# A SwiGLU feed-forward kernel: row blocks of 384, 384, 384, 384 and 512 in place of four of 512

## The chip, the cores and the metric

One core of a Trainium2 chip. The time is device microseconds of one execution. The span of a profile runs from the first to the last instruction of one profiled execution; the time is a little longer. Kernels are compared only within the same rounds.

## The reference

```
x: (1, 2048, 640)   w_gate, w_up: (640, 1536)   w_down: (1536, 640)   all bf16
return (silu(x @ w_gate) * (x @ w_up)) @ w_down
```

## The kernel before

The work is done in row blocks. For each block, twelve steps (`fc`) of gate and up projections (five matmuls each, contraction 640 = 5 x 128) fill `aT`; ScalarE takes the silu of the gate, VectorE multiplies. Then one group `po_t` gives 128 of the 640 output columns in transposed form, and one group `po_a` per 128 rows the other 512.

```
S_BLK = 512; NSB = 4; SUB = 4
W_CHUNKS = [(0, 1), (1, 3), (3, 6), (6, 9), (9, 12)]      # slices in which w_gate and w_up are loaded
# SyncE queue: x chunks, weight slices, w_down, then
turn_x(1)                       # x of block 1, transposed by the DMA
x_row <- last four rows of x, broadcast
turn_w(wgT, wgt_v)              # w_gate transposed, three slices of four fc
```

The last four rows are not in the matmuls. They are computed by VectorE as 96 row dots of `wgT` and `wuT` with `x_row`, handed out between the other work by `do_dots(n)`. In the traces here VectorE, ScalarE, TensorE and the SyncE queue take their work one after the other in the order of the program (ScalarE, for example, casts the first `po_a` at 37.41 us, behind the four stores that it began to issue at 35.38). The loop, shortened:

```
for sb in range(NSB):
    for fc in range(KF):
        proj(pg, ...); proj(pu, ...)                       # PSUM tag "gu", 4 buffers
        silu on ScalarE, product on VectorE
        if sb > 0 and fc < KF - 2: do_dots(2)
    po_t = psum.tile(..., tag="po_b")                      # 2 buffers
    ... 12 matmuls ...
    nc.scalar.copy(ot_t, po_t)
    do_dots(3)
    nc.vector.transpose(out=ot_q, in_=ot_t)
    for q in range(4): nc.scalar.dma_start(out=out2[...], in_=ot_q[...])
    for j in range(SUB):
        po_a = psum.tile([P, DA], f32, tag="po_a")         # 2 buffers
        ... 12 matmuls ...
        nc.scalar.copy(ot, po_a)
        if 0 < j: do_dots(3)
        nc.sync.dma_start(out=out2[...], in_=ot)
    if sb == 0: turn_x(2); turn_w(wuT, wut_v); turn_x(3)
```

Of the kernel before, what the change touches and what calls it, by code (L numbers as in the profile page):

```python
# [10 lines left out]
def _body(  # L11
# [8 lines left out]
    nc = tc.nc  # L20
    P = nc.NUM_PARTITIONS
    f32 = mybir.dt.float32
    bf16 = mybir.dt.bfloat16
# [9 lines left out]
    KD = D // P  # L33
    KF = F // P
    S_BLK = 512
    NSB = S // S_BLK
    SUB = S_BLK // P
    DA = 512
    Q = 32
    N_WARM, N_GAP = 18, 2  # L40
    T = 4
    WT_STEP = 4
    ROW_J = 0
    W_CHUNKS = [(0, 1), (1, 3), (3, 6), (6, 9), (9, 12)]
    assert D % P == 0 and F % P == 0 and S % S_BLK == 0 and D > DA and SUB == 4

    consts = ctx.enter_context(tc.tile_pool(name="consts", bufs=1))
    work = ctx.enter_context(tc.tile_pool(name="work", bufs=3))
# [3 lines left out]
    )  # L52

    ident = consts.tile([P, P], bf16)
    x_sb = consts.tile([P, SUB, D], bf16)
    xT = consts.tile([P, KD, S], bf16)
    wg_sb = consts.tile([P, KD, F], bf16)
    wu_sb = consts.tile([P, KD, F], bf16)
# [24 lines left out]
    def load_x(eng, c0, c1):  # L83
        eng.dma_start(out=x_sb[:, c0:c1, :], in_=x_v[:, c0:c1, :])  # L84

    def issue_order(a, b):
        tc.add_manual_dep(
            b,
            a.name,
            mybir.DependencyInfo(  # L90
                mybir.DependencyClass.NoSync, mybir.DependencyReason.DATA
            ),
            reason="issue_order",
        )
# [8 lines left out]
    silu_first = consts.tile([P, 1], f32)  # L103
    nc.vector.memset(ones[:], 1.0)  # L104

    queues = (nc.sync, nc.scalar)
    halves = ((0, KD // 2 + 1), (KD // 2 + 1, KD))
    load_x(nc.sync, 0, 1)
    first = nc.cur_bb.bb.instructions[-1]
    load_x(nc.scalar, 2, 3)  # L110


    issue_order(first, nc.cur_bb.bb.instructions[-1])
    load_x(nc.sync, 1, 2)
    load_x(nc.scalar, 3, 4)
    for dst, src in ((wg_sb, wg_v), (wu_sb, wu_v)):
        for eng, (k0, k1) in zip(queues, halves):
            eng.dma_start(out=dst[:, k0:k1, wslice(0, 1)], in_=src[:, k0:k1, wslice(0, 1)])
    load_w(nc.sync, wg_sb, wg_v, *W_CHUNKS[1])
    nc.scalar.activation(silu_first[:], ones[:, 0:1], ACT.Silu)  # L120
# [6 lines left out]
    wut_v = w_up.rearrange("d (kf p) -> d kf p", p=P)  # L127

    def turn_x(sb):
        s_sl = slice(sb * S_BLK, (sb + 1) * S_BLK)  # L130
        nc.sync.dma_start_transpose(out=xT[:, :, s_sl], in_=xt_v[s_sl])

    def turn_w(dst, src):
        for a in range(0, KF, WT_STEP):
            nc.sync.dma_start_transpose(
                out=dst[:, a : a + WT_STEP, :], in_=src[:, a : a + WT_STEP, :]
            )
# [3 lines left out]
        out=x_row[:],  # L141
        in_=x2[S - T : S, :].rearrange("t d -> (t d)").partition_broadcast(P),
    )
    turn_w(wgT, wgt_v)

    def row_dots():

# [24 lines left out]
    def do_dots(n):  # L172
        for _ in range(n):
            next(dots, None)
# [3 lines left out]
    def warm(n):  # L178
        for _ in range(n):
            nc.tensor.matmul(  # L180
                pw[:, 0:P], lhsT=ones[:], rhs=ones[:], start=True, stop=True
            )

    def transpose_chunk(c, parts):
        c_sl = slice(c * P, (c + 1) * P)
        for copy, tag, k0, k1 in parts:
            pt = psum.tile([P, k1 - k0, P], bf16, tag=tag, name="pt")
            for kd in range(k0, k1):
                nc.tensor.transpose(  # L189
                    out=pt[:, kd - k0, :],  # L190
                    in_=x_sb[:, c, kd * P : (kd + 1) * P],
                    identity=ident[:],
                )
            copy(out=xT[:, k0:k1, c_sl], in_=pt[:])  # L194

    def proj(ps, w_sb, fc, sb, c0, c1):
        for kd in range(KD):
            nc.tensor.matmul(  # L198
                ps[:, c0:c1],
                lhsT=w_sb[:, kd, fc * P : (fc + 1) * P],  # L200
                rhs=xT[:, kd, sb * S_BLK + c0 : sb * S_BLK + c1],
                start=(kd == 0),
                stop=(kd == KD - 1),
            )

    def proj_pair(ps, w_sb, fc, sb, b):


        def pair(ap):
            return ap.rearrange("p (a b c) -> p b a c", b=2, c=P)[:, b]  # L210

        for kd in range(KD):
            nc.tensor.matmul(  # L213
                pair(ps[:]),
                lhsT=w_sb[:, kd, fc * P : (fc + 1) * P],
                rhs=pair(xT[:, kd, sb * S_BLK : (sb + 1) * S_BLK]),
                start=(kd == 0),
                stop=(kd == KD - 1),
            )

    for sb in range(NSB):
        n_s = S_BLK if sb < NSB - 1 else S_BLK - T
        s_sl = slice(sb * S_BLK, sb * S_BLK + n_s)
        for fc in range(KF):
            pg = psum.tile([P, S_BLK], f32, tag="gu", name="pg", bufs=4)
            pu = psum.tile([P, S_BLK], f32, tag="gu", name="pu", bufs=4)
            if sb == 0 and fc == 0:
                dve, act = nc.vector.tensor_copy, nc.scalar.copy
                warm(N_WARM)
                transpose_chunk(0, [(dve, "po_a", 0, KD)])  # L230
                transpose_chunk(2, [(dve, "po_b", 0, KD)])
                warm(N_GAP)
                for c in (1, 3):
                    transpose_chunk(c, [(act, "po_a", 0, 2), (dve, "po_b", 2, KD)])
                warm(2)
                proj_pair(pg, wg_sb, fc, sb, 0)
                proj_pair(pg, wg_sb, fc, sb, 1)
                proj(pu, wu_sb, fc, sb, 0, S_BLK)
                keep_order(mybir.EngineType.PE)
                keep_order(mybir.EngineType.Activation)  # L240
            else:
                proj(pg, wg_sb, fc, sb, 0, n_s)
                proj(pu, wu_sb, fc, sb, 0, n_s)
            sg = work.tile([P, S_BLK], f32)
            nc.scalar.activation(sg[:, 0:n_s], pg[:, 0:n_s], ACT.Silu)  # L245
            nc.vector.tensor_tensor(  # L246
                out=aT[:, fc, s_sl], in0=sg[:, 0:n_s], in1=pu[:, 0:n_s], op=ALU.mult
            )
            if sb > 0 and fc < KF - 2:
                do_dots(2)  # L250


        n_t = (SUB if sb < NSB - 1 else SUB - 1) * P
        po_t = psum.tile([P, n_t], f32, tag="po_b", name="po_t")
        for kf in range(KF):
            nc.tensor.matmul(  # L256
                po_t[:],
                lhsT=wd_sb[:, kf, DA:D],
                rhs=aT[:, kf, sb * S_BLK : sb * S_BLK + n_t],
                start=(kf == 0),  # L260
                stop=(kf == KF - 1),
            )
        ot_t = outp.tile([P, n_t], bf16, name="ot_t")
        ot_q = outp.tile([P, n_t], bf16, name="ot_q")
        nc.scalar.copy(ot_t[:], po_t[:])  # L265
        do_dots(3)
        nc.vector.transpose(out=ot_q[:], in_=ot_t[:])  # L267
        for q in range(P // Q):
            nc.scalar.dma_start(
                out=out2[  # L270
                    sb * S_BLK : sb * S_BLK + n_t, DA + q * Q : DA + (q + 1) * Q
                ].rearrange("(i r) c -> r i c", r=Q),
                in_=ot_q[q * Q : (q + 1) * Q, :].rearrange("r (i c) -> r i c", c=Q),
            )

        for j in range(SUB):
            s0 = sb * S_BLK + j * P
            last = sb == NSB - 1 and j == SUB - 1
            po_a = psum.tile([P, DA], f32, tag="po_a", name="po_a")
            for kf in range(KF):  # L280
                nc.tensor.matmul(  # L281
                    po_a[:],
                    lhsT=aT[:, kf, s0 : s0 + P],
                    rhs=wd_sb[:, kf, 0:DA],
                    start=(kf == 0),
                    stop=(kf == KF - 1),
                )
            ot = outp.tile([P, DA], bf16, name="ot")
            nc.scalar.copy(ot[:], po_a[:])  # L289
            if 0 < j:  # L290
                do_dots(3)
            if sb == NSB - 1 and j == ROW_J:
                row_tail()
            nc.sync.dma_start(out=out2[s0 : s0 + P, 0:DA], in_=ot[:])
            if last:
                po_b = psum.tile([P, D - DA], f32, tag="po_b", name="po_b")
                for kf in range(KF):
                    nc.tensor.matmul(  # L298
                        po_b[:],
                        lhsT=aT[:, kf, s0 : s0 + P],  # L300
                        rhs=wd_sb[:, kf, DA:D],
                        start=(kf == 0),
                        stop=(kf == KF - 1),
                    )
                ot_b = outp.tile([P, D - DA], bf16, name="ot_b")
                nc.vector.tensor_copy(out=ot_b[:], in_=po_b[:])  # L306
                nc.scalar.dma_start(out=out2[s0 : s0 + P, DA:D], in_=ot_b[:])
        if sb == 0:
            turn_x(2)
            turn_w(wuT, wut_v)  # L310
            turn_x(3)
    keep_order(mybir.EngineType.DVE)
    keep_order(mybir.EngineType.SP)

# [104 lines left out]
```

## Time and profile before

| | before |
|---|---|
| time, median of the first 3 runs | 163.87 us |
| span of the profile | 162.8 us |
| TensorE busy | 159.7 us (98%) |
| VectorE busy | 111.8 us (69%) |
| first gate matmul | 5.30 us |
| first slice of `wgT` lands / first dot | 31.0 / 32.1 us |

TensorE is busy from 5.3 us to 160.7, two microseconds before the end. In a timeline, the bracket at the end of a line gives the idle time of the engine ahead of it and what ended that.

### The profile page before, as it was taken

The numbers are of one execution on the slowest core, as the hardware profiler recorded it, in microseconds if no ns is written. First come the engines' busy times: TensorE is split into PE (matmuls) and PEld (weight loads), VectorE is DVE, ScalarE is ACT, GpSimd is POOL, SyncE is SP. The second block draws the span as 40 slices with busy tenths as digits, with TensorE's granted clock in tenths as the row PEclk, the third lists the DMA queues.
The fourth block names the chain that finished last, engine by engine and source line by source line (L and its number), as shares of the span: only waits on it lengthen the run. The fifth ranks groups of instructions, "written<-read, shape, count | busy, mean of one in ns | idle before, by whom it ended". The sixth has DMA issues, their size and how long they took to land.

```text
span 162.8 us, 2081 instructions
## 1 busy us (share of the span) xinstructions
PE 159.7 (98%) x779; PEld 75.4 (46%) x779; DVE 111.8 (69%) x251; ACT 42.6 (26%) x73; POOL 0.6 (0%) x6
## 2 busy tenths in 40 slices
PE   8999999999999999999999999999999999999994
PEld 7644444444444444444444444444444444445442
DVE  2223333499559999979919999979964999993000
ACT  3322222212232222221222322221214222222121
POOL 1000000000000000000000000000000000000000
DMA  7999999993269993003110000000420000000312
GB/s 212 295 327 330 364 216 253 245 185 60 66 152 180 220 220 68 4 0 34 64 64 0 0 4 2 0 0 0 64 68 32 0 0 0 0 0 4 53 35 73
DMA packets 42585, 15.86 MB, mean 97 GB/s; under 512 B 33232, under 2 KB 42448, under 8 KB 42576
## 3 DMA queue, kind: packets, MB, share of 16 engines
q1 hardware_dynamic: 33664, 14.75, 37.2%
q10 hardware_dynamic: 8912, 0.98, 4.0%
q8 instruction: 6, 0.10, 0.3%
q14 instruction: 3, 0.02, 0.1%
HBM read 7.21 MB, written 2.62 MB: 60 GB/s over the span
## 4 chain that ended last, share of the span: by engine, by line
PE 95%; DMA 3%; SPq 0%; DVE 0%; issue 0%
PE pu L198 32%; PE pg L198 31%; PE po_a L281 25%; PE po_t L256 6%; DMA wg_sb<-in_w_gate_dram 3%; PE pg L213 1%; SPq L84 0%; PE po_b L298 0%; DVE ot_b L306 0%
## 5 line engine op out<-in xcount | busy, mean ns | idle before, releaser
L198 PE MATMUL pu<-xT,wu_sb 128*128 128x512 bf16 (+1 forms) x240 | 59.5, 379 | 0.0
L198 PE MATMUL pg<-xT,wg_sb 128*128 128x512 bf16 (+1 forms) x235 | 58.3, 379 | 0.0
L246 DVE TENSOR_TENSOR aT<-sg,pu 128x512 bf16<-128x512 f32 (+1 forms) x48 | 32.8, 683 | 32.0 <-PE pu L198 32.0
L245 ACT ACTIVATE sg<-pg 128x512 f32<-128x512 f32 (+1 forms) x48 | 28.6, 596 | 70.2 <-PE pg L198 65.7
L281 PE MATMUL po_a<-wd_sb,aT 128*128 128x512 bf16 x192 | 42.1, 379 | 0.0
L151 DVE SCALAR_TENSOR_TENSOR prod<-wgT,x_row 128x640 f32<-128x640 bf16 x48 | 39.4, 821 | 1.1
L151 DVE SCALAR_TENSOR_TENSOR prod<-wuT,x_row 128x640 f32<-128x640 bf16 x48 | 39.4, 821 | 1.0
L198 PEld LDWEIGHTS <-wu_sb 128*128 128x128 bf16 x240 | 23.5, 98 | 28.0
L198 PEld LDWEIGHTS <-wg_sb 128*128 128x128 bf16 x235 | 23.0, 98 | 27.6
L281 PEld LDWEIGHTS <-aT 128*128 128x128 bf16 x192 | 18.8, 98 | 22.5
L289 ACT CAST ot<-po_a 128x512 bf16<-128x512 f32 x16 | 9.4, 586 | 32.3 <-PE po_a L281 21.3
L256 PE MATMUL po_t<-aT,wd_sb 128*128 128x512 bf16 (+1 forms) x48 | 10.4, 366 | 0.0
L256 PEld LDWEIGHTS <-wd_sb 128*128 128x128 bf16 x48 | 4.7, 98 | 5.1
L306 DVE CAST ot_b<-po_b 128x128 bf16<-128x128 f32 x1 | 0.3, 291 | 9.9 <-PE po_b L298 9.9
L265 ACT CAST ot_t<-po_t 128x512 bf16<-128x512 f32 (+1 forms) x4 | 2.2, 560 | 11.6 <-PE po_t L256 11.6
L194 DVE COPY xT<-pt 128x640 bf16<-128x640 bf16 (+1 forms) x4 | 1.6, 425 | 3.4 <-PE pt L189 3.4
L151 DVE DVE_READ_ACCUMULATOR prod<-wuT,x_row 128x1 f32 x48 | 3.9, 82 | 0.0
L151 DVE DVE_READ_ACCUMULATOR prod<-wgT,x_row 128x1 f32 x48 | 3.9, 82 | 0.0
L267 DVE STREAM_TRANSPOSE ot_q<-ot_t 128x512 bf16<-128x512 bf16 (+1 forms) x4 | 2.7, 678 | 1.7 <-ACT ot_t L265 1.7
L180 PE MATMUL pw<-ones 128*128 128x128 bf16 x22 | 2.8, 304 | 0.4 <-DVE ones L104 0.4
L189 PE MATMUL pt<-ident,x_sb 128*128 128x128 bf16 x20 | 2.0, 268 | 0.5 <-DMA x_sb<-in_x_dram 0.5
L180 PEld LDWEIGHTS <-ones 128*128 128x128 bf16 x22 | 2.2, 143 | 0.4 <-DVE ones L104 0.4
(17 smaller groups left out, 9.0 us busy)
## 6 DMA issues: line engine op xcount, KB each, us to landing
out_dram<-ot SPq DMA_DIRECT2D x16, 128.0 KB, 1.7
wd_sb<-in_w_down_dram SPq DMA_DIRECT2D x1, 1920.0 KB, 12.6
wg_sb<-in_w_gate_dram SPq DMA_DIRECT2D x3, 480.0 KB, 7.1
wu_sb<-in_w_up_dram SPq DMA_DIRECT2D x3, 480.0 KB, 7.6
x_row<-in_x_dram SPq DMA_DIRECT2D x1, 640.0 KB, 4.8
out_dram<-ot_q ACTq DMA_DIRECT2D x12, 32.0 KB, 1.9
x_sb<-in_x_dram SPq DMA_DIRECT2D x2, 160.0 KB, 3.0
x_sb<-in_x_dram ACTq DMA_DIRECT2D x2, 160.0 KB, 3.2
```

Source lines behind the costliest of these rows:

```text
L151: nc.vector.scalar_tensor_tensor(out=prod[:], in0=wT[:, fc, :], scalar=1.0, in1=x_row[:, t, :], op0=ALU.mult, op1=ALU.mult, accum_out=acc[ ...
L180: nc.tensor.matmul(pw[:, 0:P], lhsT=ones[:], rhs=ones[:], start=True, stop=True)
L189: nc.tensor.transpose(out=pt[:, kd - k0, :], in_=x_sb[:, c, kd * P : (kd + 1) * P], identity=ident[:],)
L198: nc.tensor.matmul(ps[:, c0:c1], lhsT=w_sb[:, kd, fc * P : (fc + 1) * P], rhs=xT[:, kd, sb * S_BLK + c0 : sb * S_BLK + c1], start=(kd == 0 ...
L213: nc.tensor.matmul(pair(ps[:]), lhsT=w_sb[:, kd, fc * P : (fc + 1) * P], rhs=pair(xT[:, kd, sb * S_BLK : (sb + 1) * S_BLK]), start=(kd == ...
L245: nc.scalar.activation(sg[:, 0:n_s], pg[:, 0:n_s], ACT.Silu)
L246: nc.vector.tensor_tensor(out=aT[:, fc, s_sl], in0=sg[:, 0:n_s], in1=pu[:, 0:n_s], op=ALU.mult)
L256: nc.tensor.matmul(po_t[:], lhsT=wd_sb[:, kf, DA:D], rhs=aT[:, kf, sb * S_BLK : sb * S_BLK + n_t], start=(kf == 0), stop=(kf == KF - 1),)
L265: nc.scalar.copy(ot_t[:], po_t[:])
L267: nc.vector.transpose(out=ot_q[:], in_=ot_t[:])
L281: nc.tensor.matmul(po_a[:], lhsT=aT[:, kf, s0 : s0 + P], rhs=wd_sb[:, kf, 0:DA], start=(kf == 0), stop=(kf == KF - 1),)
L289: nc.scalar.copy(ot[:], po_a[:])
```

## The change

The intent is a shorter head: a first block of three chunks needs one x load and five transposes less before its first matmul. The first weight slices are cut finer, since a smaller block wants them faster, and the last two `wgT` slices move behind the first block.

```diff
-    S_BLK = 512
+    SUBS = [3, 3, 3, 3, 4]                  # chunks of 128 rows
-    W_CHUNKS = [(0, 1), (1, 3), (3, 6), (6, 9), (9, 12)]
+    W_CHUNKS = [(0, 1), (1, 2), (2, 4), (4, 6), (6, 9), (9, 12)]
 ...
-    load_x(nc.scalar, 3, 4)                 # the fourth x chunk of the first block
 ...
-    turn_w(wgT, wgt_v)
+    turn_w(wgT, wgt_v, 0, WT_STEP)          # the first slice only
 ...
-            if sb > 0 and fc < KF - 2:
-                do_dots(2)
+            if sb > 0 and (SUBS[sb] == 3 or fc < KF - 2):
+                do_dots(SUBS[sb] - 2)
 ...
         if sb == 0:
+            turn_w(wgT, wgt_v, WT_STEP, KF)
             turn_x(2)
-            turn_w(wuT, wut_v)
+            turn_w(wuT, wut_v, 0, KF)
             turn_x(3)
+            turn_x(4)
```

Cut: the same index changes wherever a block is addressed; the first gate group, now chunks 0 and 2 and then chunk 1; which of the two queues loads which part of the very first weight slices; and a fixed issue order of the first two x loads, which is dropped.

More of the change, by code (lines that the diff above doesn't have):

```diff
@@ L35, in _body @@
     S_BLK = 512
-    NSB = S // S_BLK
-    SUB = S_BLK // P
+    SUBS = [3, 3, 3, 3, 4]
+    NSB = len(SUBS)
+    ROW0 = [sum(SUBS[:n]) * P for n in range(NSB)]
     DA = 512
@@ L43, in _body @@
     ROW_J = 0
-    W_CHUNKS = [(0, 1), (1, 3), (3, 6), (6, 9), (9, 12)]
-    assert D % P == 0 and F % P == 0 and S % S_BLK == 0 and D > DA and SUB == 4
+    W_CHUNKS = [(0, 1), (1, 2), (2, 4), (4, 6), (6, 9), (9, 12)]
+    assert D % P == 0 and F % P == 0 and S == sum(SUBS) * P and D > DA and max(SUBS) * P <= S_BLK
     consts = ctx.enter_context(tc.tile_pool(name="consts", bufs=1))
@@ L54, in _body @@
     ident = consts.tile([P, P], bf16)
-    x_sb = consts.tile([P, SUB, D], bf16)
+    x_sb = consts.tile([P, SUBS[0], D], bf16)
     xT = consts.tile([P, KD, S], bf16)
@@ L104, in _body @@
     nc.vector.memset(ones[:], 1.0)
-    queues = (nc.sync, nc.scalar)
-    halves = ((0, KD // 2 + 1), (KD // 2 + 1, KD))
     load_x(nc.sync, 0, 1)
-    first = nc.cur_bb.bb.instructions[-1]
     load_x(nc.scalar, 2, 3)
-    issue_order(first, nc.cur_bb.bb.instructions[-1])
     load_x(nc.sync, 1, 2)
-    load_x(nc.scalar, 3, 4)
-    for dst, src in ((wg_sb, wg_v), (wu_sb, wu_v)):
-        for eng, (k0, k1) in zip(queues, halves):
+    for dst, src, k in ((wg_sb, wg_v, 3), (wu_sb, wu_v, 2)):
+        for eng, k0, k1 in ((nc.scalar, 0, k), (nc.sync, k, KD)):
             eng.dma_start(out=dst[:, k0:k1, wslice(0, 1)], in_=src[:, k0:k1, wslice(0, 1)])
@@ L129, in turn_x, with turn_w @@
     def turn_x(sb):
-        s_sl = slice(sb * S_BLK, (sb + 1) * S_BLK)
+        s_sl = slice(ROW0[sb], ROW0[sb] + SUBS[sb] * P)
         nc.sync.dma_start_transpose(out=xT[:, :, s_sl], in_=xt_v[s_sl])
-    def turn_w(dst, src):
-        for a in range(0, KF, WT_STEP):
+    def turn_w(dst, src, lo, hi):
+        for a in range(lo, hi, WT_STEP):
             nc.sync.dma_start_transpose(
@@ L194, in transpose_chunk, with proj @@
             copy(out=xT[:, k0:k1, c_sl], in_=pt[:])
-    def proj(ps, w_sb, fc, sb, c0, c1):
+    def proj(ps, w_sb, fc, sb, n, cols=lambda ap: ap):
         for kd in range(KD):
             nc.tensor.matmul(
-                ps[:, c0:c1],
+                cols(ps[:, 0:n]),
                 lhsT=w_sb[:, kd, fc * P : (fc + 1) * P],
-                rhs=xT[:, kd, sb * S_BLK + c0 : sb * S_BLK + c1],
+                rhs=cols(xT[:, kd, ROW0[sb] : ROW0[sb] + n]),
                 start=(kd == 0),
@@ L204, in proj, with outer_chunks, mid_chunk @@
             )
-    def proj_pair(ps, w_sb, fc, sb, b):
-        def pair(ap):
-            return ap.rearrange("p (a b c) -> p b a c", b=2, c=P)[:, b]
-        for kd in range(KD):
-            nc.tensor.matmul(
-                pair(ps[:]),
-                lhsT=w_sb[:, kd, fc * P : (fc + 1) * P],
-                rhs=pair(xT[:, kd, sb * S_BLK : (sb + 1) * S_BLK]),
-                start=(kd == 0),
-                stop=(kd == KD - 1),
-            )
+    def outer_chunks(ap):
+        return ap.rearrange("p (c r) -> p c r", r=P)[:, 0:3:2]
+    def mid_chunk(ap):
+        return ap[:, P : 2 * P]
     for sb in range(NSB):
-        n_s = S_BLK if sb < NSB - 1 else S_BLK - T
-        s_sl = slice(sb * S_BLK, sb * S_BLK + n_s)
+        n_s = SUBS[sb] * P - (T if sb == NSB - 1 else 0)
+        s_sl = slice(ROW0[sb], ROW0[sb] + n_s)
         for fc in range(KF):
@@ L232, in _body @@
                 warm(N_GAP)
-                for c in (1, 3):
-                    transpose_chunk(c, [(act, "po_a", 0, 2), (dve, "po_b", 2, KD)])
-                warm(2)
-                proj_pair(pg, wg_sb, fc, sb, 0)
-                proj_pair(pg, wg_sb, fc, sb, 1)
-                proj(pu, wu_sb, fc, sb, 0, S_BLK)
+                transpose_chunk(1, [(act, "po_a", 0, 2), (dve, "po_b", 2, KD)])
+                warm(N_GAP)
+                proj(pg, wg_sb, fc, sb, n_s, outer_chunks)
+                proj(pg, wg_sb, fc, sb, n_s, mid_chunk)
+                proj(pu, wu_sb, fc, sb, n_s)
                 keep_order(mybir.EngineType.PE)
@@ L241, in _body @@
             else:
-                proj(pg, wg_sb, fc, sb, 0, n_s)
-                proj(pu, wu_sb, fc, sb, 0, n_s)
+                proj(pg, wg_sb, fc, sb, n_s)
+                proj(pu, wu_sb, fc, sb, n_s)
             sg = work.tile([P, S_BLK], f32)
@@ L248, in _body @@
             )
-            if sb > 0 and fc < KF - 2:
-                do_dots(2)
-        n_t = (SUB if sb < NSB - 1 else SUB - 1) * P
+            if sb > 0 and (SUBS[sb] == 3 or fc < KF - 2):
+                do_dots(SUBS[sb] - 2)
+        n_t = (SUBS[sb] if sb < NSB - 1 else SUBS[sb] - 1) * P
         po_t = psum.tile([P, n_t], f32, tag="po_b", name="po_t")
@@ L258, in _body @@
                 lhsT=wd_sb[:, kf, DA:D],
-                rhs=aT[:, kf, sb * S_BLK : sb * S_BLK + n_t],
+                rhs=aT[:, kf, ROW0[sb] : ROW0[sb] + n_t],
                 start=(kf == 0),
@@ L270, in _body @@
                 out=out2[
-                    sb * S_BLK : sb * S_BLK + n_t, DA + q * Q : DA + (q + 1) * Q
+                    ROW0[sb] : ROW0[sb] + n_t, DA + q * Q : DA + (q + 1) * Q
                 ].rearrange("(i r) c -> r i c", r=Q),
@@ L274, in _body @@
             )
-        for j in range(SUB):
-            s0 = sb * S_BLK + j * P
-            last = sb == NSB - 1 and j == SUB - 1
+        for j in range(SUBS[sb]):
+            s0 = ROW0[sb] + j * P
+            last = sb == NSB - 1 and j == SUBS[sb] - 1
             po_a = psum.tile([P, DA], f32, tag="po_a", name="po_a")
```

## The prediction

> **What bounds the kernel now.** I read the chain of work that ended last first, since it says which engine sets the end and where the end is not that engine.
>
> ```profile
> PE 95%; DMA 3%; SPq 0%; DVE 0%; issue 0%
> 0.91 4.35 DMA wg_sb<-in_w_gate_dram
> 5.30 1.27 PE pg L213 x10
> 31.39 2.59 PE po_t L256 x12
> 33.98 10.36 PE po_a L281 x48
> 147.74 1.95 PE po_t L256 x12
> 149.69 10.36 PE po_a L281 x48
> ```
>
> The kernel is a TensorE stream. It starts at 5.30 us, when the first gate weights have landed, and then runs without a hole until 160.7; the rest is the last copy and store. So there are two ways to move the time: start the stream earlier, or open a hole in it. The second matters as much as the first, so I next read what works beside TensorE at the end of the first row block, in the timeline:
>
> ```profile
> 31.50 0.69 DVE L246 TENSOR_TENSOR aT<-sg,pu 128x512 bf16<-128x512 f32 x1 [1.47 <-PE pu L198]
> 32.10 0.82 DVE L151 SCALAR_TENSOR_TENSOR prod<-wgT,x_row 128x640 f32<-128x640 bf16 x1
> 34.63 0.71 DVE L267 STREAM_TRANSPOSE ot_q<-ot_t 128x512 bf16<-128x512 bf16 x1
> 35.38 1.99 ACTq L269 DMA_DIRECT2D out_dram<-ot_q  x4
> 37.41 0.59 ACT L289 CAST ot<-po_a 128x512 bf16<-128x512 f32 x1 [2.81 <-DMA out_dram<-ot_q]
> ```
>
> This is a chain of its own. VectorE does three row dots (32.10 to 34.63), then its transpose; ScalarE issues the stores of the transposed tile only after that (35.38), and only then casts the first `po_a` (37.41). `po_a` has two buffers, so the third group of `po_a` matmuls waits for that cast. Before, the cast ends at 38.00 and the third group is due at 33.98 + 2 x 2.59 = 39.16: a slack of 1.2 us that the chain of waits never shows. Last I read when the dots' inputs arrive, from the SyncE timeline and the list of DMA issues:
>
> ```profile
> 10.66 1.43 SPq L125 DMA_DIRECT2D wd_sb<-in_w_down_dram  x1
> 12.13 11.32 SPq L131 DMA_TRANSPOSE xT<-in_x_dram  x1
> 23.50 0.57 SPq L140 DMA_DIRECT2D x_row<-in_x_dram  x1
> 24.12 4.39 SPq L135 DMA_TRANSPOSE wgT<-in_w_gate_dram  x1
> wgT<-in_w_gate_dram SPq DMA_TRANSPOSE x1, 6.9
> ```
>
> The first slice of `wgT` lands at 24.12 + 6.9 = 31.0 us. VectorE wants it at 32.10. So the dots do not wait today, by 1.1 us. The table by windows shows why it cannot come much sooner: the DMA engines are at a busy share of about 1.0 to 1.2 from 2 us to 20 us, at 255 to 364 GB/s, and the SyncE queue sends everything in order: x, weights, `wd`, transposed x, `x_row`, `wgT`.
>
> **What the Trainium skill says.** "TensorE: Matmul & The Clock Gate", section "Wait — 56ns, not 53.3ns?", gives N / 2.4 GHz + 2.5 ns from matmul to matmul: 216 ns at 512 columns, 162.5 at 384. The trace agrees: 2.59 us / 12 = 216 ns, and the last block's `po_t` of 384 columns 1.95 / 12 = 162.5 ns. "PSUM — Partial Sum Buffer", section "Engine vs sequencer instructions", says that ScalarE and VectorE queues are strict FIFO and that matmuls start in program order. The trace agrees: ScalarE stood 2.81 us behind its store with a finished `po_a` waiting. "DMA: Bandwidth & Descriptors", section "Issuing engines are not separate DMA queues", says that all DMAs share the same 16 engines; the busy share agrees, and so moving slices between the two queues does not make `wgT` come earlier. The first page's section "What's actually happening" says that TensorE falls to half clock after about one idle window of 3.4 us and needs about as long to come back. The head agrees with a cold start (ten transposes took 1.27 us from 2.28 and 0.76 us from 4.23); no trace here has yet an idle stretch later.
>
> **The change, part by part.**
>
> Matmul columns. Gate and up matmuls go from 480 of 512 columns to 480 of 384 and 120 of 512 (508 in the last block), `po_t` from 48 to 60; columns are the same. 132 more matmuls at 2.5 ns each are +0.3 us.
>
> Head. x loads go from four to three and the five transposes and the copies of the fourth chunk go. Ahead of the last needed x chunk each queue still carries 320 KB or so (two x chunks on one; one x chunk and two weight slices on the other), so that chunk lands near 4.2 us as now (wait at 4.23). Then five transposes and two fillers (0.5 us), and the gate weights, with 160 KB less ahead of them, land before 5. I take the first gate matmul at 4.7, an estimate, against 5.30; the first group also loses some 0.2 us less to waits. GpSimd does the same four constants and the same identity as before in the order of instructions: nothing is gained there. The gain of the head is 0.6 to 0.8 us, if it reaches the end.
>
> Weights for the first block. An fc step takes 10 x 162.5 ns = 1.62 us instead of 2.16, so weights are wanted a quarter sooner. Laying the bytes along the measured rates gives about 0.4 us of slack at the tightest slice (`wu` of step 2, landing near 8.4) and about 1 us for `wd` (near 23.2, wanted at 24.3). No hole is expected, but it is close.
>
> End of the first block. TensorE comes to `po_t` at 4.7 + 1.7 + 11 x 1.62 = 24.2 us instead of 31.4, to `po_a` at 26.2, and wants the third `po_a` at 26.2 + 5.2 = 31.4. VectorE wants its first dot at about 25. The order of instructions shows that the three dots still stand ahead of the transpose, and the four stores ahead of the `po_a` casts. `wgT`, though, comes only a little sooner: 31.0, less 0.5 for the 160 KB of x that is gone, less 0.7 for the quarter less of transposed x (2.66 us of issue for a full one later in the trace), plus 0.2 for finer and so slower slices: 30.0. From there: three dots 2.53 us (32.10 to 34.63), 384-column transpose to first store 0.61 (150.24 to 150.85 in the last block), stores to cast 1.98 (150.85 to 152.83), cast 0.59, sum 5.7. The third `po_a` starts at 35.7 instead of 31.4: a hole of 4.3 us in the stream. Its end is set by DMA, so the head's gain is swallowed by it.
>
> The rest. Block 1 starts at 35.7 + 2.59 = 38.3. Blocks 1 to 3 take 120 x 0.1625 + 1.95 + 36 x 0.216 = 29.2 each, 87.7. In these, VectorE has per step a product (0.55, scaled from 0.69) and one dot (0.87), 1.4 of 1.62 us: it does not fall behind. Their third `po_a` is close (one dot more stands ahead of the transpose than before: the cast ends some 7.2 us after the last up matmul, the third group is due at 7.1), worth up to 0.1 each. The last block is as before, from 122.04 to 162.8: 40.8. Sum 38.3 + 87.7 + 40.8 = 166.8 of span against 162.8; the median stands 1.1 above the span, so 167.9. A hole of 4.3 us holds a whole idle window of 3.4 in about one case in three ((4.3 - 3.4) / 3.4), which would cost some 1.7 us more (half speed for 3.4 us): +0.5 on average. I say 168.2.
>
> **The rivals.**
> 1. The hole is not there, or small: `wgT` comes in time and the head's gain stays. Then 163.87 - 0.7 + 0.3 = 163.5. For it: the change takes the second and third `wgT` slices out of the way, as if its author had watched this queue. Against it: the first slice would have to land 4 us sooner, with 320 KB less of some 8,300 KB ahead of it on a saturated queue.
> 2. The hole is there but shorter, since the queue is cleared faster than I reckon (no later transposes behind the first slice, no cost of finer slices). Landing at 29.0 makes 166.9, just inside 2%.
> 3. The hole is there and the clock goes cold after it: 169.6 to 170.
> 4. Weights arrive late in the first block. This only moves TensorE's wait forward into the same hole, since the hole ends when `wgT` has landed; the end stays near 168.
>
> **Range and chances.** The landing of `wgT` moves the end one for one; give it 1 us either way, add the cold clock above: 166.2 to 170.4. The limit for slower by over 2% is 167.1; the landing would have to be over 0.8 us sooner than reckoned. I give slower 0.70, same 0.29, faster 0.01: the head alone is worth under 0.5%.
>
> **What would show it.** Right: a TensorE idle stretch of about 4 us near 31 to 36 us ahead of the third `po_a`, released by ScalarE; VectorE idle from about 25 to 30 us ahead of its first dot, released by the `wgT` or `x_row` DMA; first gate matmul near 4.7; 384-column groups of five at 0.81 us; blocks 1 to 3 without holes over 0.2. Wrong: `wgT` landed by 26 us, or a first dot that starts right after the last product of block 0, or holes in the weights' loads in block 0 that push TensorE past the landing.

## The result, and the profile after

| | before | after |
|---|---|---|
| time, median of 6 | 163.91 us | 171.12 us (168.8 to 172.12) |
| ratio, fast runs | 1 | 1.0378 (1.0313 to 1.0442) |
| span of the profiled run | 162.8 us | 168.9 us |
| TensorE clock | 1.00 (profiled run) | 1.00 in one of the six runs, 0.98 to 0.99 in five |
| time less span | 1.3 us (profiled run) | 1.6 us |

A ratio is the mean time of one kernel's fast runs over that of the other's of the same rounds, so not quite the ratio of the medians. Three of the six runs count as slow (over 1.5% above the fastest, 171.3 to 172.1 us); the three fast ones are 168.8, 170.56 and 170.9. The experiments show what such a spread is made of. The change is slower by 3.8% by the fast runs, and by 4.4% by the medians of all six; since the spread turns out to belong to the change, both are fair readings.

The chain of work that ended last, changed kernel (start, duration, what):

```profile
PE 74%; SPq 11%; DMA 6%; DVE 5%; ACTq 2%; issue 1%; ACT 1%; DVEq 0%
...
23.52 6.12 DMA wgT<-in_w_gate_dram
...
29.74 0.84 DVE prod L145 x2
...
32.30 0.50 DVE ot_q L251
32.83 0.36 ACTq L253
...
34.79 0.59 ACT ot L273
35.43 4.09 PE po_a L265 x12
39.52 1.16 PE pg L192 x5
40.68 0.81 PE pu L192 x5
```

TensorE's share of the chain fell from 95% to 74%. Up to 35 us the chain is no longer TensorE but the SyncE queue, then the `wgT` transpose, then the dots, VectorE's transpose, ScalarE's stores and its cast. Only then does TensorE take over. The timeline of the same kernel shows both ends of that:

```profile
29.74 0.82 DVE L145 SCALAR_TENSOR_TENSOR prod<-wgT,x_row 128x640 f32<-128x640 bf16 x1 [4.25 <-DMA wgT<-in_w_gate_dram]
...
35.43 4.09 PE L265 MATMUL po_a<-wd_sb,aT 128*128 128x512 bf16 x12 [3.47 <-ACT ot L273]
...
66.66 2.75 PE L265 MATMUL po_a<-wd_sb,aT 128*128 128x512 bf16 x12 [0.16 <-ACT ot L273]
```

VectorE stood 4.25 us until `wgT` came, TensorE 3.47 us until ScalarE had emptied the first `po_a`. The third line is the same place in the next block: a wait of 0.16 us that comes back there. Twelve such matmuls take 2.75 us by this view (the last one's modelled end included), but 4.09 just after the hole. The table by windows says why (window, its length, TensorE busy, weight load, VectorE, ScalarE, GpSimd, granted clock, DMA share, GB/s):

```profile
33.20:36.60 3.40, 1.17 (x6) 0.57 (x6) 3.26 (x9) 1.07 (x2) 0.00 (x0) 1.00 0.38 60
36.60:40.00 3.40, 3.40 (x11) 1.27 (x10) 1.22 (x4) 0.44 (x1) 0.00 (x0) 0.51 0.17 51
40.00:42.00 2.00, 2.00 (x14) 1.21 (x13) 0.40 (x1) 0.63 (x2) 0.00 (x0) 0.98 0.22 71
```

From 36.6 to 40.0 us the granted clock is half. The drop comes 1.2 us after TensorE had resumed, and lasts 3.4 us. It cost 4.09 - 2.59 = 1.5 us in the third group and 1.16 - 0.81 = 0.35 in the next.

### The profile page after: what moved, and what is told of

Same layout as the page of the kernel before. It is cut to its first block, busy times and chain, and to the rows that moved or that the text cites. A ratio compares the mean times of both kernels' runs of the same rounds, so it can differ in the third digit from the quotient of the medians.

```text
span 168.9 us, 2402 instructions
## 1 busy us (share of the span) xinstructions
PE 162.8 (96%) x906; PEld 89.1 (53%) x906; DVE 113.5 (67%) x263; ACT 44.2 (26%) x85; POOL 0.6 (0%) x6
## 4 chain that ended last, share of the span: by engine, by line
PE 74%; SPq 11%; DMA 6%; DVE 5%; ACTq 2%; issue 1%; ACT 1%; DVEq 0%
PE pg L192 25%; PE pu L192 25%; PE po_a L265 20%; SPq L125 6%; SPq L82 4%; DMA wgT<-in_w_gate_dram 4%; PE po_t L240 3%; DVE prod L145 3%; ACTq L253 2%; DMA wg_sb<-in_w_gate_dram 2%; SPq L119 1%; ACT ot L273 1%; DVE ot_q L251 1%; PE po_b L282 0%; SPq L134 0%
## 5 line engine op out<-in xcount | busy, mean ns | idle before, releaser
L192 PE MATMUL pg<-xT,wg_sb 128*128 128x384 bf16 (+3 forms) x305 | 62.8, 339 | 0.0
L192 PE MATMUL pu<-xT,wu_sb 128*128 128x384 bf16 (+1 forms) x300 | 61.7, 336 | 0.0
L230 DVE TENSOR_TENSOR aT<-sg,pu 128x384 bf16<-128x384 f32 (+1 forms) x60 | 34.7, 579 | 36.3 <-PE pu L192 36.3
L229 ACT ACTIVATE sg<-pg 128x384 f32<-128x384 f32 (+1 forms) x60 | 30.7, 512 | 70.1 <-PE pg L192 70.1
L265 PE MATMUL po_a<-wd_sb,aT 128*128 128x512 bf16 x192 | 44.2, 387 | 3.7 <-ACT ot L273 3.6
L192 PEld LDWEIGHTS <-wg_sb 128*128 128x128 bf16 x305 | 30.4, 100 | 23.4 <-issue 0.9
L192 PEld LDWEIGHTS <-wu_sb 128*128 128x128 bf16 x300 | 29.4, 98 | 22.4
L240 PE MATMUL po_t<-aT,wd_sb 128*128 128x384 bf16 x60 | 10.6, 326 | 0.0
L249 ACT CAST ot_t<-po_t 128x384 bf16<-128x384 f32 x5 | 2.4, 479 | 11.5 <-PE po_t L240 11.5
L251 DVE STREAM_TRANSPOSE ot_q<-ot_t 128x384 bf16<-128x384 bf16 x5 | 2.9, 572 | 0.0
```

What stands on the lines that cost most here:

```text
L192: nc.tensor.matmul(cols(ps[:, 0:n]), lhsT=w_sb[:, kd, fc * P : (fc + 1) * P], rhs=cols(xT[:, kd, ROW0[sb] : ROW0[sb] + n]), start=(kd == 0 ...
L229: nc.scalar.activation(sg[:, 0:n_s], pg[:, 0:n_s], ACT.Silu)
L230: nc.vector.tensor_tensor(out=aT[:, fc, s_sl], in0=sg[:, 0:n_s], in1=pu[:, 0:n_s], op=ALU.mult)
L240: nc.tensor.matmul(po_t[:], lhsT=wd_sb[:, kf, DA:D], rhs=aT[:, kf, ROW0[sb] : ROW0[sb] + n_t], start=(kf == 0), stop=(kf == KF - 1),)
L251: nc.vector.transpose(out=ot_q[:], in_=ot_t[:])
L265: nc.tensor.matmul(po_a[:], lhsT=aT[:, kf, s0 : s0 + P], rhs=wd_sb[:, kf, 0:DA], start=(kf == 0), stop=(kf == KF - 1),)
```

## The experiments

Eight kernels were run, on two chips (e1 to e4, then e5 to e8); the kernel before ran beside them (medians 164.32 in the first, 163.92 in the second). All gave correct results.

**e1: no dots ahead of the first transpose.**

```diff
-        do_dots(3)
+        if sb > 0:
+            do_dots(3)
         nc.vector.transpose(out=ot_q[:], in_=ot_t[:])
```

> The changed kernel without the three row dots ahead of the first block's transpose (they are made up for at the end). Theory (the dots wait for the first wgT slice, and the transpose, the four stores, the cast and the third po_a group wait behind them): the TensorE hole of 3.5 us at 32 to 35.4 goes, and with it the stretch of half clock after it; 163.0 to 163.8 us, ratio to before 0.995 to 1.0. Rival (blocks of 384 rows or the finer loads are slower by themselves): 167 us or more, and the hole closes only to open elsewhere.

Measured: 165.25 us (165.12 to 165.33), ratio 1.0067 (1.0045 to 1.009), clock 1.00 in all six runs. Timeline of e1:

```profile
26.75 7.72 PE L266 MATMUL po_a<-wd_sb,aT 128*128 128x512 bf16 x35
...
30.16 0.83 DVE L145 SCALAR_TENSOR_TENSOR prod<-wgT,x_row 128x640 f32<-128x640 bf16 x1 [2.35 <-DMA wgT<-in_w_gate_dram]
```

`wgT` comes as late as in the changed kernel (30.16 against 29.74) and VectorE still waits for it, but behind the transpose now, where nobody waits for VectorE: the `po_a` groups of block 0 run through (one record is missing). The hole and the half clock are gone, and the scatter with them. Against expectation the kernel is not level with the one before: the ratio is 1.0067, and at most 1.000 was expected. So a part of the loss is not the hole.

**e2: a third `po_a` buffer, with the dots where they were.**

```diff
-        po_a = psum.tile([P, DA], f32, tag="po_a", name="po_a")
+        po_a = psum.tile([P, DA], f32, tag="po_a", name="po_a", bufs=3)
```

(and one buffer instead of two for `po_b`, which keeps the number of PSUM buffers at eight; one transposed tile of the head moves from `po_b` to `po_a`.)

> The changed kernel with three po_a buffers and one po_b buffer; the dots still wait for wgT and the transpose and the casts still come late. Theory (the wait reaches TensorE only through the third po_a buffer): no hole ahead of the third po_a group, though VectorE is still idle to about 29.7; up to 0.5 us may come back as a wait of block 1 for the late first product; 163.3 to 164.5 us. Rival (TensorE waits for something else that lands then): the hole stays, 168 us or more.

Measured: 165.12 us (164.73 to 165.2), ratio 1.0054 (1.0028 to 1.008), clock 1.00. Timeline of e2:

```profile
26.66 7.72 PE L265 MATMUL po_a<-wd_sb,aT 128*128 128x512 bf16 x35
...
30.42 0.83 DVE L145 SCALAR_TENSOR_TENSOR prod<-wgT,x_row 128x640 f32<-128x640 bf16 x1 [5.10 <-DMA wgT<-in_w_gate_dram]
...
39.05 0.97 PE L192 MATMUL pu<-xT,wu_sb 128*128 128x384 bf16 x5 [0.59 <-DVE aT L230]
```

VectorE waits even longer, 5.10 us, and TensorE does not mind: the wait reached it through the third `po_a` buffer alone. As expected some of it (0.59 us, and a little of `issue` at the weight loads) comes back in block 1, where the first product is late. The time was 0.6 us over the upper end expected.

**e3: the first `wgT` slice sent ahead of the transposed x of block 1.**

```diff
-    turn_x(1)
     x_row <- ...
     turn_w(wgT, wgt_v, 0, WT_STEP)
+    turn_x(1)
```

> The changed kernel with the transposed x of block 1 sent after x_row and the first wgT slice instead of ahead of them. Theory: wgT lands 1.5 to 2.2 us sooner (27.5 to 28.2 against 29.7), the hole shrinks one for one to 1.3 to 2.0 us, which is under an idle window, so the clock stays at 1.00: 164.6 to 166.0 us. Rival (the hole's end does not follow wgT): 168 us or more.

Measured: two runs at 167.38 and 167.41 us with clock 1.00, two at 169.35 and 169.58 with clock 0.99; ratio over all 1.026. The trace is of a run at clock 1.00:

```profile
28.26 0.83 DVE L145 SCALAR_TENSOR_TENSOR prod<-wgT,x_row 128x640 f32<-128x640 bf16 x1 [2.82 <-DMA wgT<-in_w_gate_dram]
...
33.96 2.75 PE L265 MATMUL po_a<-wd_sb,aT 128*128 128x512 bf16 x12 [2.04 <-ACT ot L273]
```

The first dot comes 1.48 us sooner than in the changed kernel, and the third `po_a` group 1.47 us sooner. The times are 1.4 us and more over what was expected, partly for the same unexplained rest as in e1, partly since two runs met the half clock with a hole that was expected to be too short for it. (The "idle window" of the expectation is the 3.4 us that the prediction takes from the Trainium skill.) Those two have no trace.

**e4: the hole filled with idle matmuls.** Fifteen matmuls of 512 columns into a spare PSUM tile ahead of the third `po_a` group of block 0:

```diff
+            if sb == 0 and j == 1:
+                pf = psum.tile([P, S_BLK], f32, tag="gu", name="pf", bufs=4)
+                for _ in range(15):
+                    nc.tensor.matmul(pf[:], lhsT=ones[:], rhs=wd_sb[:, 0, 0:DA], start=True, stop=True)
```

> The changed kernel with 15 idle matmuls of 512 columns (3.2 us) put where the hole is, ahead of the third po_a group. Theory (part of the loss is TensorE's half clock after the idle hole, and it makes the runs scatter): the third group still starts near 35.5, but runs at full clock (2.6 us instead of 4.1): 168.0 to 169.0 us, with a scatter under 0.5 us. Rival (the slow stretch after the hole has another cause, such as weights or buffers): still 2 us of slow matmuls after 35.5 and 170 us or more.

Measured: 169.4 us (168.94 to 170.47), clock 1.00 in all four runs. Timeline of e4 (of its slowest run):

```profile
31.20 0.83 DVE L145 SCALAR_TENSOR_TENSOR prod<-wgT,x_row 128x640 f32<-128x640 bf16 x1 [5.80 <-DMA wgT<-in_w_gate_dram]
31.70 3.40 PE L275 MATMUL pf<-wd_sb,ones 128*128 128x512 bf16 x15
36.90 2.53 PE L265 MATMUL po_a<-wd_sb,aT 128*128 128x512 bf16 x11 [1.79 <-ACT ot L279]
```

Kept busy, TensorE keeps its clock: the third group runs at 2.53 us for eleven records. But the scatter of 1.5 us did not go and the median is 0.4 us over the upper end expected, a miss. In this run `wgT` came 1.46 us later than in the changed kernel's trace (first dot 31.20 against 29.74), and the third group as much later. Over the traces of the kernels that leave the order of the SyncE queue as it is (changed, e1, e2, e4, e6, and e7 with coarser slices), VectorE waits for `wgT` until between 29.74 and 31.20 us. So the spread has two sources: when `wgT` lands, and whether the half clock follows. That the first makes the scatter of e4 is argued, since its other three runs have no trace. Because of it, this run alone doesn't give the price of the half clock.

**e8: e3 with nine idle matmuls in its hole.**

> The run that sent wgT first (two of its runs 167.4 at clock 1.00, two 169.5 at 0.99), with nine idle matmuls of 512 columns (1.9 us) in its hole of 2 us. Theory (the two levels are the half clock after the hole, which comes in some runs only): all runs at clock 1.00 and 167.2 to 167.7 us. Rival (the two levels come from the loads): still two levels 2 us apart.

Measured: 167.76, 167.82, 167.82 and 168.39 us, clock 1.00 in all four; ratio 1.0251 (1.0231 to 1.0271). The upper level of e3 (clock 0.99) does not come up, so it was the half clock; its price in e3 is 169.5 - 167.4 = 2.1 us. The times lie 0.06 to 0.7 us over the range expected, a small miss, and the lower level came out 0.4 us above e3's. In its trace the first dot is at 28.55 us and the third group at 34.24, both 0.3 later than in e3's. The two ran on different chips, so the levels can't be compared more finely than that.

**e5: the same chain in the kernel before.** The `wgT` slices are sent in another order; nothing else changes, all blocks are 512.

```diff
-    turn_w(wgT, wgt_v)
+    for a in (4, 8, 0):
+        nc.sync.dma_start_transpose(out=wgT[:, a : a + WT_STEP, :], in_=wgt_v[:, a : a + WT_STEP, :])
```

> The kernel before, blocks of 512 and all, with only the order of the three wgT slices turned (second, third, first), so that the slice of the first dots lands some 5.5 us later, near 36.6 instead of 31.0. Theory (the chain wgT, dots, transpose, stores, cast, third po_a group is in the kernel before too, with 1.1 us to spare at its head and 1.2 us at its end): first dot near 36.6, cast done near 42.5, third po_a group 3.2 us late; with the clock full 167 us, with the half clock after the hole 169. Rival (the hole belongs to blocks of 384): within 0.5 us of the kernel before.

Measured: 170.15 us (169.51 to 171.13), ratio 1.0406 (1.0373 to 1.0438), clock 0.98 to 0.99 in all runs. Timeline of e5:

```profile
36.83 0.82 DVE L154 SCALAR_TENSOR_TENSOR prod<-wgT,x_row 128x640 f32<-128x640 bf16 x1 [4.39 <-DMA wgT<-in_w_gate_dram]
...
42.71 7.03 PE L284 MATMUL po_a<-wd_sb,aT 128*128 128x512 bf16 x24 [3.29 <-ACT ot L292]
```

A hole of 3.29 us (3.2 expected), at the predicted place, and 24 matmuls in 7.03 us instead of 5.34. The time is 1.1 us over the 169 expected with the half clock; the traced run, the fastest, is 0.5 over it. One late slice in the kernel before costs as much as the whole change did. The hole doesn't belong to blocks of 384.

Over the five traces that keep both links of the chain (dots ahead of the transpose, two `po_a` buffers), the time from the first dot to the start of the third `po_a` group:

| kernel | first dot | third group | difference |
|---|---|---|---|
| changed | 29.74 | 35.43 | 5.69 |
| e3 | 28.26 | 33.96 | 5.70 |
| e8 | 28.55 | 34.24 | 5.69 |
| e4 | 31.20 | 36.90 | 5.70 |
| e5 (512 columns) | 36.83 | 42.71 | 5.88 |

**e6: fewer dots ahead of VectorE's transpose, in all blocks.** No dots ahead of it in block 0, one in the later blocks, the other two behind the stores.

```diff
-        do_dots(3)
+        do_dots(1 if sb > 0 else 0)
         nc.vector.transpose(out=ot_q[:], in_=ot_t[:])
         ... stores ...
+        do_dots(2 if sb > 0 else 0)
```

> The changed kernel with no dots ahead of the first block's transpose, and one instead of three ahead of the later ones (the other two follow the stores). Theory: the hole of the first block goes as in the run without dots ahead, and the waits of 0.16 us ahead of the third po_a group in blocks 1 to 3 go too; span 163.5 less 0.5, so 164.6 us, some 0.4 to 0.5 us under the run without dots ahead and level with the kernel before (ratio 1.000 to 1.004). Rival (the 0.16 us are not waits but belong to the matmuls): the same 165.2 as that run.

Measured: 164.8 us (164.2 to 165.13), ratio 1.0053 (1.0034 to 1.0073). Timeline of e6, `po_a` of block 1:

```profile
56.19 7.93 PE L266 MATMUL po_a<-wd_sb,aT 128*128 128x512 bf16 x36
```

The group of 36 runs through, where the changed kernel and e1 have a wait of 0.16 us before the last twelve. From `po_t` to the next `po_t`, every block of 384 takes 29.22 us here. In e1 the same stretches take 29.54 (53.80 to 83.34) and 29.40 (83.34 to 112.74), and in the changed kernel as well (59.20 to 88.74 to 118.14). So these are waits, of 0.32 us in block 1 and about 0.18 in blocks 2 and 3, some 0.7 us in all; the bracket in the timeline shows less, since it starts at the modelled end of the last matmul. In time the two runs can't be set against each other exactly: the ratios differ by 0.14%, with overlapping intervals, and the head of e6's trace came 0.4 us later than e1's. Still slower than before, by 0.5%; a ratio of at most 1.004 was expected.

**e7: e6 with the coarse weight slices of before.**

```diff
-    W_CHUNKS = [(0, 1), (1, 2), (2, 4), (4, 6), (6, 9), (9, 12)]
+    W_CHUNKS = [(0, 1), (1, 3), (3, 6), (6, 9), (9, 12)]
```

> The same kernel as the one with the transposes first, with the coarser weight slices of before (1 to 3, 3 to 6, 6 to 9, 9 to 12). Theory (the first block's end is set by the rate of the weights' loading, not by the start of the stream, so the slicing shifts the waits but the first block ends near 24.7 either way): within 0.4 us of it. Rival (the finer slices earn their place): 1 us slower or more, with waits for weights of step 1 in the first block.

Measured: 164.84 us (164.72 to 165.04), ratio 1.0063 (1.0049 to 1.0077): the same as e6. Timeline of e7:

```profile
4.21 0.98 PE L192 MATMUL pg<-xT,wg_sb 128*128 128x256 bf16 x10
...
5.87 0.66 PE L192 MATMUL pu<-xT,wu_sb 128*128 128x384 bf16 x3 [0.28 <-DMA wu_sb<-in_w_up_dram]
6.96 0.99 PE L192 MATMUL pg<-xT,wg_sb 128*128 128x384 bf16 x5 [0.42 <-DMA wg_sb<-in_w_gate_dram]
```

TensorE starts at 4.21 us, over a microsecond sooner than before, and then waits for weights. In this form the finer slices earn nothing that these runs can show. The first block ended at 25.14 us here and at 25.02 in e6, 0.3 to 0.4 later than expected.

**Where the head's gain went.** The start of `po_t` in block 0 measures the head and the first block together. In the kernel before it is at 31.23 us; taking off 53.3 ns for each of the 120 matmuls (215.8 - 162.5, 6.4 us in all) for the narrower block leaves 24.83. The others (e5 has the head of before, and the same is taken off):

| kernel | first gate matmul | `po_t` of block 0 | what lay between |
|---|---|---|---|
| before | 5.30 | 24.83 | first gate group 1.27 us |
| e5 | 4.97 | 25.08 | group at 1.86 us |
| changed | 4.38 | 24.66 | group at 1.76 us |
| e1 | 4.61 | 24.58 | group at 1.41 us; then a weight load waits 0.25 us, the matmuls hardly |
| e2 | 4.36 | 24.49 | group at 0.98 us, then waits for weights |
| e3 | 4.54 | 24.62 | group at 1.56 us |
| e4 | 4.46 | 24.57 | group at 0.98 us, then waits for weights |
| e6 | 4.53 | 25.02 | group at 1.81 us, the next one 0.2 us long too |
| e7 | 4.21 | 25.14 | group at 0.98 us, then waits for weights |
| e8 | 4.48 | 24.22 | group at 1.21 us, no wait of the matmuls |

With the changed head the stream starts 0.7 to 1.1 us sooner than in the trace of before, and arrives between 0.3 us later and 0.6 sooner; the mean of the eight is 24.66, against 24.95 for the two with the old head. Either the matmuls of the first group run long, or they run at full speed and then wait for weights. The waits of e4, a run of the second kind, as its timeline shows them at the weight loads:

```profile
8.00 0.60 PEld L192 LDWEIGHTS <-wg_sb 128*128 128x128 bf16 x5 [0.51 <-DMA wg_sb<-in_w_gate_dram]
9.12 0.60 PEld L192 LDWEIGHTS <-wu_sb 128*128 128x128 bf16 x5 [0.52 <-DMA wu_sb<-in_w_up_dram]
```

Of the first kind is the changed kernel. By form, the five 256-column matmuls of the changed kernel's head have a mean of 421 ns, those of before 274:

```profile
L192 PE MATMUL pg<-xT,wg_sb 128*128 128x256 bf16 x5 | 1.3, 421 | 0.0
L213 PE MATMUL pg<-xT,wg_sb 128*128 128x256 bf16 x10 | 1.3, 274 | 0.2 <-DMA wg_sb<-in_w_gate_dram 0.2
```

From the start of this group to that of the next it is 1.59 us in the changed kernel and 0.82 in e2, where the same ten matmuls run at full speed: near double. That fits a TensorE still on the half clock it begins with, while in the trace of before the clock had risen by then. It is not a matter of the kernel alone: e5, with the old head, has a slow first group too. That this is the clock is argued from the durations; the granted clock recorded in the head is 1.00 in both.

## Why the prediction was right

The range of 166.2 to 170.4 us holds the mean of the three fast runs (170.09), not the median of all six (171.12). Some of its figures don't follow from its own terms: 167.9 and 0.5 make 168.4, not 168.2; (4.3 - 3.4) / 3.4 is one case in four, not in three; and 1 us either way with the cold clock makes 166.9 to 170.6. And of the 2.81 us that ScalarE "stood behind its store with a finished `po_a` waiting", only the last 0.8 had one: the first group ended at 33.98 + 2.59 = 36.57 us, the cast began at 37.41. None of this touches the argument. By its steps:

- **The hole: right.** It is where it was predicted, with the predicted releasers on VectorE and TensorE. e1 and e2 take away one link each and it goes; e5 makes it in the kernel before.
- **Its end: right, 35.43 against 35.7.** The landing was reckoned at 30.0; the first dot started at 29.74. The 5.7 us from the first dot to the third group were measured as 5.69.
- **Its width: 3.6 against 4.3.** TensorE was due at the third group at 26.61 + 5.18 = 31.8 instead of 31.4 (the idle time shown, 3.47, starts at a modelled end), since the first gate group took 1.76 us. As predicted, that moved nothing but the start of the hole.
- **The head's gain of 0.6 to 0.8 us: wrong.** The first gate matmul came even sooner than the 4.7 us reckoned (4.38), but without the hole the gain should have shown in e1, e6 and e7. It did not: the table above leaves 0.3 us on average. The step took an earlier first matmul for an earlier stream. It reckoned with a full-speed first group, and with 0.4 us of slack in the weights: `wu` of step 2 landing at 8.4 us and wanted at 4.7 + 1.7 + 1.62 + 0.81 = 8.83. In e1, e2, e4 and e8 the weight load waited for that slice until 9.13, 9.04, 9.12 and 8.74. So the slack was about nil, and an earlier start only finds a wait there. This also made rival 1 too low: 163.5 is 0.2% under the kernel before, and without the hole the change measures 0.5 to 0.7% over it.
- **The half clock: the mechanism was right, the term mis-sized.** It was put at one case in three, an estimate from the page's 3.4 us for a hole that must hold a whole idle window. It came in five of six runs, in all four of e5, and in two of four of e3, with a hole of 2.04 us in the one run of e3 that has a trace. Its cost, 1.85 us in the profiled run, was near the 1.7 reckoned. The one run at clock 1.00 took 168.8, the other five 170.6 to 172.1.
- **Blocks 1 to 3: 87.7 predicted, 88.7 measured** (39.52 to 128.20). The half clock's tail is 0.35 of the difference, the waits for the third `po_a` 0.7. They were put at up to 0.1 each. e6 without them has 29.22 a block, as predicted.
- **More matmuls, +0.3 us: fits.** A group of five at 384 columns takes 0.81 us in the chain. No run took this term alone.
- **Time less span: missed.** It was taken as 1.1 us; it is 1.3 in the kernel before and 1.6 in the changed kernel and its variants.

For the profiled run the terms add up: 167.9 reckoned without the half clock, 1.85 for it, 0.7 for the waits in blocks 1 to 3 and 0.5 outside the span, less 0.4 for a hole that ended sooner and a last block that was shorter, make 170.55 against 170.56 measured. The waits and the part outside the span were not foreseen at this size. That they fitted into the range, beside a half clock that came in most runs, is luck.

The rest of e6 against before, 0.9 us, is in size 0.3 for the matmuls, 0.3 outside the span, and about 0.2 for a head that came late in that trace. It is a sum that fits, not a set of separate tests.

## What to carry to other kernels

When a change makes one engine reach a point earlier, list what else is due at that point and when it arrives by itself: here TensorE came 7 us earlier to a place whose data was bound by a full DMA queue, and the spare 1.1 us in VectorE's wait was nowhere in the chain that ended last. In an in-order queue, put work whose data may be late behind work that others wait for; taking three dots from ahead of a transpose (they are made up for later) took out the whole hole. And count the start of a stream as a gain only if what feeds its next steps comes earlier too.

## What the Trainium skill lacked or had wrong

- "TensorE: Matmul & The Clock Gate", section "What's actually happening", puts the fall to half clock after at least one idle window of about 3.4 us. Here it fell 1.2 us after TensorE had resumed from 3.47 idle, so the 3.4 us ahead of the fall held 1.17 us of busy TensorE. It came in all four runs of e5, with a hole of 3.29 us in the traced one, and in two of four of e3 (169.4 and 169.6 us against 167.4), where the traced run, one of the other two, had a hole of 2.04 us. In the four runs of e4, with 1.79 us idle in the traced one, it did not come. So a stretch that is only partly idle seems to be enough; how much idle it takes, and whether the fall lags behind the stretch that caused it, no run here shows. The length of the half-clock time, 3.4 us, agrees with the page.
- The page on TensorE warns that clock events in a trace can be unreliable, but no page says that the granted clock of a profile doesn't show the slow start: it reads 1.00 from 0 us, while five 256-column matmuls at 4.4 us took 421 ns each, against 274 in the kernel before.
- No page says what makes the time outside the span differ between kernels: it is 1.27 to 1.37 us in every listed run of the kernel before and of e5 (2081 instructions in the profile), and 1.57 to 1.66 in every run of the changed kernel and its variants (2397 to 2426). With two levels only, that it goes by the number of instructions is not shown.
